# A cosformer attention and SwiGLU kernel: loads as casts on one queue, PSUM banks from one ring, the second batch woven into the first group, groups of 512 tokens

## The chip, the core and the metric

One Trainium2 chip, one NeuronCore. The metric is the device time of one execution in microseconds (us). The kernel before takes 384.12 us, the median of three runs (383.35 to 384.22).

## What is computed

```python
# q, k, v: [8 batches, 8 heads, 576 positions, 64], float32
q_p = concat(relu(q) * cos_w, relu(q) * sin_w)       # cos and sin of the position, 128 features
k_p = concat(relu(k) * cos_w, relu(k) * sin_w)
kv  = einsum('bhsf,bhsd->bhfd', k_p, v)
z   = sum(k_p, axis=2)
num = einsum('bhsf,bhfd->bhsd', q_p, kv)
x   = num / (einsum('bhsf,bhf->bhs', q_p, z) + 1e-6)  # -> 4608 tokens x 512
g   = x @ w_gate                                      # 512 x 1536
out = (silu(g) * (x @ w_val)) @ w_out                 # 1536 x 512, float32 out
```

## The kernel before

**Layout.** The 576 positions of a batch are cut into NC = 9 slots of 64 positions, slot c holding the positions p * 9 + c. The 8 heads go as 4 pairs g, one head of a pair on partitions 0 to 63, the other on 64 to 127. The 8 x 9 = 72 slots follow one another as the token axis of the feed-forward part. It is cut by `bounds` (L42) into nine groups: the first has 9 slots (576 tokens), seven have 8 (512 tokens), the last has 7 (448 tokens).

**Attention of one batch.** `relu` (L142) makes the relu of q and k as bf16 copies, `vcast` (L151) a bf16 copy of v, `vmul` (L156) multiplies v by the table of cosines and sines. `kv_mm` (L187) accumulates the kv products in PSUM (two calls of 36 matmuls), `kv_out` (L203) copies them out. q is transposed by DMA (`qturn_dma`, L168) or on TensorE (`qturn_pe`, L174). Then tiles of two slots (128 tokens; one slot where a group or the batch ends) are made: `a_half` (L220) makes four heads of a tile with four matmuls, an eviction on ScalarE (`tmp`, L239) and one on VectorE (`num`, L241), and there are ten halves to a batch; `x_norm` (L246) divides, with three VectorE operations; `x_turn` (L260) transposes the tile into `xT`, on TensorE and ScalarE if `fast`, else by a DMA transpose from SP's queue.

**Feed-forward of one group.** `ffn_fc` (L311) makes 128 of the 1536 hidden features for a range of tokens: four matmuls with w_gate and four with w_val into a pair of PSUM banks, Silu on ScalarE (`sg`), a product on VectorE into `ht` (L330). `ffn_out` (L336) makes 128 tokens of the output with twelve matmuls, an eviction that alternates between ScalarE and VectorE, and two stores from SP's queue.

**PSUM.** Three pools: `ps_f` has two buffers of two banks (feed-forward, transposes of q, the fast halves), `ps_o` two of one bank (outputs, transposes of x), `ps_a` one of two banks (kv products and all other halves).

**Order.** The program is emitted in the order in which each engine runs it. Batch 0's attention comes first (`features_fast(0)`, L355, then `tiles_fast`, L292). Batch 1's features (`features_fast(1)`) stand between the second and third output tile of group 0 (L417), and its tiles ahead of group 1. In groups 0 and 1 each `ffn_fc` is split into a first part of 4 slots (256 tokens) and the rest. The work of batches 2 to 7 is put into slots of a plan (`at`, L363): a group has 12 slots after its `ffn_fc` and 4 after its output tiles, SLOTS = 16. The table at L369 says at which slot of the plan the features of a batch begin and how many steps go into a slot, when q is transposed (`tq`), when the kv products are made (`tk`), and how many halves go into one slot (`hn`, from tk + 3 on).

**Loads.** k, v and q of batch 0 come as float32 by the queues of ScalarE and SP. A small copy on GpSimd (`hold`, L122) waits for q; behind it GpSimd's queue loads the weights, cast to bf16 by the DMA, and then batch after batch as float32 (two buffers per tensor).

Of the kernel before, what the change touches and what calls it, by code (L numbers as in the profile page):

```python
# [17 lines left out]
def kernel(  # L18
# [28 lines left out]
    raw = ctx.enter_context(tc.tile_pool(name="raw", bufs=2))  # L47
# [26 lines left out]

    load(0, "k", [nc.scalar], 2)
    load(0, "v", [nc.sync], 2)
    load(0, "q", [nc.scalar, nc.sync], 2)


    def angles(name, step):  # L80
        it = consts.tile([P, NC], mybir.dt.int32, name=f"{name}_i")
        for e in range(2):
            nc.gpsimd.iota(it[e * SH:(e + 1) * SH], pattern=[[1, NC]], base=e * step, channel_multiplier=NC)
        pos = consts.tile([P, NC], FP32, name=f"{name}_p")
        nc.vector.tensor_copy(out=pos, in_=it)
        return pos

    ident = consts.tile([P, P], BF16)
    pos_k = angles("k", 0)
    pos_t = angles("t", 1)  # L90
    halfpi = consts.tile([P, 1], FP32)
    nc.vector.memset(halfpi, math.pi / 2.0)
    zerob = consts.tile([P, 1], FP32)
    nc.vector.memset(zerob, 0.0)
    rad = math.pi / 2.0 / S
    csk = consts.tile([P, NC, 2], FP32)
    cst = consts.tile([P, NC, 2], FP32)
    for cs, pos in ((csk, pos_k), (cst, pos_t)):
        nc.scalar.activation(out=cs[:, :, 0], in_=pos, func=AF.Sin, scale=-rad, bias=halfpi[:])
        nc.scalar.activation(out=cs[:, :, 1], in_=pos, func=AF.Sin, scale=rad, bias=zerob[:])  # L100
    tiny = consts.tile([P, 1], FP32)
    nc.scalar.activation(out=tiny, in_=zerob, func=AF.Silu)
# [4 lines left out]
    )  # L107
    v2s = []
# [4 lines left out]
    make_identity(nc, ident)  # L113
# [5 lines left out]
    hold = consts.tile([P, 2], FP32)  # L119

    def load_weights():
        nc.gpsimd.tensor_copy(out=hold, in_=raws[0, "q"][:, 1:G:2, NC - 1, D - 1])  # L122
        wg_r = moe_w_gate.rearrange("(c p) f -> p c f", p=P)
        wv_r = moe_w_val.rearrange("(c p) f -> p c f", p=P)
        wo_r = moe_w_out.rearrange("(c p) f -> p c f", p=P)
        f0 = 0
        for n in (2, 2, 4, 4):
            fs = slice(f0 * P, (f0 + n) * P)
            f0 += n
            nc.gpsimd.dma_start(out=wg_sb[:, :, fs], in_=wg_r[:, :, fs])  # L130
            nc.gpsimd.dma_start(out=wv_sb[:, :, fs], in_=wv_r[:, :, fs])
        for i in range(3):
            cs = slice(4 * i, 4 * i + 4)
            nc.gpsimd.dma_start(out=wo_sb[:, cs], in_=wo_r[:, cs])
# [4 lines left out]
    def copy(i, out, in_):  # L139
        (nc.scalar.copy if i % 2 == 0 else nc.vector.tensor_copy)(out=out, in_=in_)  # L140

    def relu(b, nm, g, fast=False):  # L142
        if g == 0:
            st[b, nm] = rel.tile([P, J, NC, 2, D] if nm == "q" else [P, G, NC, D], BF16, name=f"r_{nm}")
        o = st[b, nm][:, g // 2, :, g % 2] if nm == "q" else st[b, nm][:, g]
        if fast:
            nc.vector.tensor_single_scalar(out=o, in_=raws[b, nm][:, g], scalar=0.0, op=ALU.max)  # L147
        else:
            nc.scalar.activation(out=o, in_=raws[b, nm][:, g], func=AF.Relu)  # L149

    def vcast(b, g, fast=False):  # L151
        t = rel.tile([P, NC, D], BF16, name="vb")
        st[b, "vb", g] = t
        (nc.gpsimd.tensor_copy if fast else nc.scalar.copy)(out=t, in_=raws[b, "v"][:, g])  # L154

    def vmul(b, g):  # L156
        nc.vector.tensor_tensor(  # L157
            out=v2s[b % 2][:, g, :, :, 0:D],
            in0=st.pop((b, "vb", g)).unsqueeze(2).to_broadcast([P, NC, 2, D]),
            in1=tab, op=ALU.mult,  # L160
        )
# [12 lines left out]
    def qturn_pe(b, j):  # L174
        qt = qt_of(b)
        ps = ps_f.tile([P, 2, 8, P], BF16, name="qt_ps", tag="f")
        for c in range(NC):
            nc.tensor.transpose(  # L178
                out=ps[:, c // 5, c % 5],
                in_=st[b, "q"][:, j, c].rearrange("p i d -> p (i d)"),  # L180
                identity=ident,
            )
        for i, (c0, n) in enumerate(((0, 5), (5, 4))):
            copy(i, qt[:, :, j, c0:c0 + n].rearrange("p e c s -> p c e s"),
                 ps[:, i, 0:n].rearrange("p c (e s) -> p c e s", e=2))

    def kv_mm(b, j):  # L187
        if j == 0:
            st[b, "kvps"] = ps_a.tile([P, 2, 512], FP32, name="kv_ps", tag="att")
        ps = st[b, "kvps"]  # L190
        for c in range(NC):
            for i in range(2):
                for e in range(2):
                    es = slice(e * SH, (e + 1) * SH)
                    g = 2 * j + i
                    nc.tensor.matmul(  # L196
                        out=ps[i * D:(i + 1) * D, e, j * 2 * D1:(j + 1) * 2 * D1],
                        lhsT=st[b, "k"][es, g, c],
                        rhs=v2s[b % 2][es, g, c, :, 0:D1],
                        start=(c == 0), stop=(c == NC - 1),  # L200
                    )

    def kv_out(b):  # L203
        kvs = kvp.tile([P, 2, J, 2 * D1], BF16, name="kvs")
        nc.scalar.copy(out=kvs.rearrange("p e j x -> p e (j x)"), in_=st.pop((b, "kvps"))[:, :, 0:J * 2 * D1])
# [4 lines left out]
    def tiles_of(b):  # L210
        cut = next((g - b * NC for g in bounds if b * NC < g < (b + 1) * NC), NC)
# [8 lines left out]
    def a_half(b, c, n, j, fast=False):  # L220
# [3 lines left out]
        ps = (ps_f if fast else ps_a).tile([P, 2, 512], FP32, name="a_ps", tag="f" if fast else "att")  # L224
        av = ps[0:m, :, 0:4 * D1].rearrange("p i (w e x) -> p i w e x", w=2, e=2)
# [9 lines left out]
        if j == 0:  # L235
            st[b, "num", c] = smp.tile([P, H, D1], FP32, name="num", bufs=3)
# [23 lines left out]
    def x_turn(b, c, n, fast=False):  # L260
        m = n * SH
        x = st.pop((b, "x", c))
        idx = b * NC + c
        tg = max(t for t in range(NTG) if bounds[t] <= idx)
        if tg not in xT:
            xT[tg] = xtp.tile([P, KC, 9 * SH], BF16, name="xT")
        off = (idx - bounds[tg]) * SH
        o = xT[tg][:, :, off:off + m]
        if fast:
            ps = ps_o.tile([P, KC, P], BF16, name="xt_ps", tag="o")  # L270
# [3 lines left out]
            nc.scalar.copy(out=o, in_=ps[:, :, 0:m])  # L274
        else:
            nc.sync.dma_start_transpose(out=o, in_=x[0:m])

    def features_fast(b):
        for g in range(G):
            vcast(b, g, fast=True)  # L280
        for g in range(G):
            relu(b, "k", g, fast=True)
            vmul(b, g)
        for j in range(J):
            kv_mm(b, j)
        for g in range(G):
            relu(b, "q", g)
        kv_out(b)
        for j in range(J):
            qturn_pe(b, j)  # L290

    def tiles_fast(b, fill):  # L292

        ts = tiles_of(b)
        fill = list(fill)
        for t, (c, n) in enumerate(ts):
            for j in range(J):
                a_half(b, c, n, j, fast=True)
            if t > 0:
                x_turn(b, *ts[t - 1], fast=True)  # L300
            x_norm(b, c, n)
            if t > 1:
                fill.pop(0)()
        x_turn(b, *ts[-1], fast=True)
        for f in fill:
            f()
# [4 lines left out]
    def ffn_fc(tg, fc, lo=0, hi=None, mid=None):  # L311

        hi = bounds[tg + 1] - bounds[tg] if hi is None else hi
# [3 lines left out]
        ps = ps_f.tile([P, 2, 512], FP32, name="f_ps", tag="f")  # L317
        for half, w in ((0, wg_sb), (1, wv_sb)):
            for kc in range(KC):
                nc.tensor.matmul(out=ps[:, half, 0:n], lhsT=w[:, kc, fs], rhs=xT[tg][:, kc, ts],  # L320
                                 start=(kc == 0), stop=(kc == KC - 1))
            if half == 0 and mid is not None:
                mid()
# [127 lines left out]
```

## Time and profile before

| | us |
|---|---|
| median of three runs | 384.12 |
| the profiled execution, as a run | 384.02 |
| its span, first to last instruction | 382.2 |
| TensorE busy in it | 339.3 (89%) |
| VectorE busy | 200.2 (52%) |
| ScalarE busy | 172.4 (45%) |
| GpSimd busy | 33.4 (9%) |

The span is what the trace shows; 1.8 us of the time lie around it. Matmuls are pipelined, so that the rows of one matmul overlap those of the next: the distance between two starts is its cost, not the duration printed. Idle time of an engine costs something only where the engine that ends the kernel waits for it. PE is TensorE, PEld its weight loads, DVE VectorE, ACT ScalarE, POOL GpSimd, SP the engine that issues stores and DMA transposes.

### The profile page before, as it was taken

What the parts mean: (1) busy time and instruction counts of PE and PEld (TensorE: products, weight loads), DVE (VectorE), ACT (ScalarE), POOL (GpSimd) and SP (SyncE); (2) the same over time, 40 slices, a digit from 0 to 9 for tenths busy, and PEclk for the clock granted to TensorE, in tenths of its full rate; (3) what the DMA queues carried; (4) which work ended last, traced back from release to release, by engine and by line L of the source; (5) the groups of instructions that cost most, each with busy time, mean ns of one, the idle gap of its engine ahead of it and who ended that gap; (6) DMA issues with size and microseconds to landing.
All of it is one profiled execution on the core that took longest, in us unless ns stands there. A gap on an engine that the chain in (4) does not pass through costs nothing.

```text
span 382.2 us, 6246 instructions
## 1 busy us (share of the span) xinstructions
PE 339.3 (89%) x2428; PEld 171.0 (45%) x2460; DVE 200.2 (52%) x461; ACT 172.4 (45%) x339; POOL 33.4 (9%) x54
## 2 busy tenths in 40 slices
PE   0679996858896789999999999999999999999995
PEld 0446663525673344344444444444444444444542
DVE  4564445275555654863595378447744753432321
ACT  3644333244754546743673376347533522321320
POOL 3842301200020020001001000000000000000000
PEclk9999999788998999999999999999999999999999
DMA  8899982740246378199219905501550133003013
GB/s 297 159 199 208 413 335 55 277 150 0 63 157 242 72 200 311 27 153 343 97 36 180 379 16 73 133 17 21 91 124 2 29 78 68 0 21 90 2 23 87
DMA packets 47981, 49.95 MB, mean 131 GB/s; under 512 B 30800, under 2 KB 36432, under 8 KB 47952
## 3 DMA queue, kind: packets, MB, share of 16 engines
q0 software_dynamic: 11568, 29.49, 25.2%
q1 hardware_dynamic: 35568, 18.29, 22.2%
q10 hardware_dynamic: 816, 1.77, 1.2%
q8 instruction: 19, 0.31, 0.3%
q14 instruction: 10, 0.08, 0.1%
HBM read 37.75 MB, written 9.44 MB: 123 GB/s over the span
## 4 chain that ended last, share of the span: by engine, by line
PE 81%; DVE 9%; ACT 4%; DMA 2%; issue 2%; ACTq 0%; DVEq 0%
PE f_ps L320 48%; PE o_ps L341 24%; PE a_ps L229 4%; PE kv_ps L196 3%; DVE ht L330 2%; DMA raw_k<-in_k_dram 2%; DVE v L157 2%; DVE num L241 2%; ACT sg L325 2%; DVE x L254 1%; PE qt_ps L178 1%; ACT tmp L239 1%; PE xt_ps L272 1%; DVE r_k L147 1%; DVE ob L140 1%
## 5 line engine op out<-in xcount | busy, mean ns | idle before, releaser
L330 DVE TENSOR_TENSOR ht<-sg,f_ps 128x192 bf16<-128x192 bf16 (+5 forms) x192 | 81.5, 451 | 100.4 <-ACT sg L325 100.2
L325 ACT ACTIVATE sg<-f_ps 128x512 bf16<-128x512 f32 (+3 forms) x132 | 68.5, 519 | 123.9 <-PE f_ps L320 109.3
L320 PE MATMUL f_ps<-xT,wg_sb 128*128 128x512 bf16 (+3 forms) x518 | 118.1, 348 | 6.1 <-DVE ht L330 3.8
L320 PE MATMUL f_ps<-xT,wv_sb 128*128 128x512 bf16 (+3 forms) x522 | 116.5, 347 | 0.0
L341 PE MATMUL o_ps<-wo_sb,ht 128*128 128x512 bf16 x416 | 97.6, 384 | 1.3 <-issue 0.6
L320 PEld LDWEIGHTS <-wv_sb 128*128 128x128 bf16 x528 | 52.9, 100 | 43.2
L320 PEld LDWEIGHTS <-wg_sb 128*128 128x128 bf16 x528 | 47.5, 100 | 46.2 <-DVE ht L330 7.2
L341 PEld LDWEIGHTS <-ht 128*128 128x128 bf16 x432 | 41.2, 99 | 49.7 <-issue 2.8
L241 DVE SCALAR_TENSOR_TENSOR num<-a_ps,cst,tmp 128x260 f32<-128x260 f32 (+1 forms) x80 | 38.2, 482 | 16.6 <-ACT tmp L239 16.2
L239 ACT ACTIVATE tmp<-a_ps,cst 128x260 f32<-128x260 f32 (+1 forms) x80 | 37.4, 473 | 20.6 <-PE a_ps L229 19.6
L229 PE MATMUL a_ps<-kvs,qt 64*128 64x130 bf16 (+1 forms) x320 | 24.7, 237 | 11.9 <-DVE num L241 8.2
L157 DVE TENSOR_TENSOR v<-vb,tab 128x1152 bf16<-128x1152 bf16 x32 | 25.9, 810 | 9.8 <-ACT vb L154 9.5
L140 DVE COPY ob<-o_ps 128x512 f32<-128x512 f32 x18 | 12.4, 690 | 35.2 <-PE o_ps L341 35.2
L229 PEld LDWEIGHTS <-qt 64*128 64x128 bf16 (+1 forms) x320 | 11.4, 99 | 39.8 <-issue 37.2
L254 DVE TENSOR_TENSOR x<-num,rec 128x512 bf16<-128x512 f32 (+1 forms) x40 | 27.6, 690 | 1.4
L140 ACT COPY ob<-o_ps 128x512 f32<-128x512 f32 x18 | 10.5, 585 | 37.9 <-PE o_ps L341 35.7
L196 PE MATMUL kv_ps<-v,r_k 64*64 64x130 bf16 x576 | 14.6, 241 | 14.6 <-DVE v L157 14.6
L149 ACT ACTIVATE r_q<-raw_q 128x576 bf16<-128x576 f32 x32 | 20.7, 676 | 6.0 <-DMA raw_q<-in_q_dram 6.0
L196 PEld LDWEIGHTS <-r_k 64*64 64x64 bf16 x576 | 11.7, 119 | 20.2 <-issue 10.5
L73 POOL DMA_DIRECT2D raw_k<-in_k_dram x8 | 5.9, 741 | 133.0 <-ACT r_k L149 127.2
L149 ACT ACTIVATE r_k<-raw_k 128x576 bf16<-128x576 f32 x24 | 16.3, 677 | 0.0
L154 ACT CAST vb<-raw_v 128x576 bf16<-128x576 f32 x24 | 16.0, 667 | 0.0
(39 smaller groups left out, 83.1 us busy)
## 6 DMA issues: line engine op xcount, KB each, us to landing
out_dram<-ob SPq DMA_DIRECT2D x72, 128.0 KB, 2.4
raw_k<-in_k_dram POOLq DMA_DIRECT2D x6, 1152.0 KB, 6.9
raw_v<-in_v_dram POOLq DMA_DIRECT2D x6, 1152.0 KB, 9.0
raw_q<-in_q_dram POOLq DMA_DIRECT2D x6, 1152.0 KB, 11.3
wo_sb<-in_moe_w_out_dram POOLq DMA_DIRECT2D x3, 512.0 KB, 18.0
raw_k<-in_k_dram ACTq DMA_DIRECT2D x2, 576.0 KB, 6.7
raw_v<-in_v_dram SPq DMA_DIRECT2D x2, 576.0 KB, 6.4
raw_k<-in_k_dram POOLq DMA_DIRECT2D x2, 576.0 KB, 18.4
```

What stands on the lines that cost most here:

```text
L140: (nc.scalar.copy if i % 2 == 0 else nc.vector.tensor_copy)(out=out, in_=in_)
L149: nc.scalar.activation(out=o, in_=raws[b, nm][:, g], func=AF.Relu)
L157: nc.vector.tensor_tensor(out=v2s[b % 2][:, g, :, :, 0:D], in0=st.pop((b, "vb", g)).unsqueeze(2).to_broadcast([P, NC, 2, D]), in1=tab, op= ...
L196: nc.tensor.matmul(out=ps[i * D:(i + 1) * D, e, j * 2 * D1:(j + 1) * 2 * D1], lhsT=st[b, "k"][es, g, c], rhs=v2s[b % 2][es, g, c, :, 0:D1] ...
L229: nc.tensor.matmul(out=av[:, i, :, e], lhsT=qt[hs, e, j, c:c + n].rearrange("p c s -> p (c s)"), rhs=kvs[hs, e, j].rearrange("p (w x) -> p ...
L239: nc.scalar.activation(out=tmp[0:m], in_=av[:, :, 0].rearrange("p i e x -> p i (e x)"), func=AF.Copy, scale=cst[0:m, c, 0:1])
L241: nc.vector.scalar_tensor_tensor(out=nv, in0=av[:, :, 1].rearrange("p i e x -> p i (e x)"), scalar=cst[0:m, c, 1:2], in1=tmp[0:m], op0=ALU ...
L254: nc.vector.tensor_tensor(out=x[0:m].rearrange("p (h d) -> p h d", h=H), in0=num[0:m, :, 0:D], in1=rec[0:m].to_broadcast([m, H, D]), op=AL ...
L320: nc.tensor.matmul(out=ps[:, half, 0:n], lhsT=w[:, kc, fs], rhs=xT[tg][:, kc, ts], start=(kc == 0), stop=(kc == KC - 1))
L325: nc.scalar.activation(out=sg[:, 0:n], in_=ps[:, 0, 0:n], func=AF.Silu)
L330: nc.vector.tensor_tensor(out=ht[:, fc, r:r + w], in0=sg[:, at_:at_ + w], in1=ps[:, 1, at_:at_ + w], op=ALU.mult)
L341: nc.tensor.matmul(out=o_ps, lhsT=ht[:, fc, r:r + P], rhs=wo_sb[:, fc], start=(fc == 0), stop=(fc == FC - 1))
```

## The change

- Groups are 8 slots each (`GH`), all nine of 512 tokens. `ht` holds two groups.
- k, v and q are loaded as bf16, cast by the DMA, all from GpSimd's queue with three buffers per tensor; only k of batch 0 comes as float32 from SP's queue. The order on GpSimd's queue is: v of batch 0, q of batch 0 (slots 0 to 3, then 4 to 8), weights of `ffn_fc` 0 to 7, k of batch 1, weights of 8 to 11, v of batch 1, the first slots of q of batch 1, w_out, the rest of q of batch 1, batch 2. `hold` and `vcast` are gone, and the relu of k is made in place.
- All of PSUM is one tile of 8 banks. `take` gives them out in a ring, one or an aligned pair at a time, and skips banks that are held (kv products until copied out, outputs until complete).
- `qturn_pe` transposes raw q, and its eviction makes the relu.
- For batch 0 two tiles are made ahead of the first `ffn_fc`, two more between the first six half-width `ffn_fc` of group 0, the last in group 0's slots 2 to 4. Only group 0 is split into halves of 256 tokens.
- Batch 1's features stand in slots 3 to 11 of group 0; its first eight halves, their turns and the rest of q's transposes stand between thirds of group 0's four output tiles; its last tile is in group 1.
- For batch 2, `hn` goes from 2 to 1, and the features of a batch are 8 steps and no longer 12.

```diff
-    bounds = [0, 9] + [9 + 8 * i for i in range(1, 8)] + [NH]
-    NTG = len(bounds) - 1
-    R = 6 * P
+    GH = 8
+    T = GH * SH
+    NTG = NH // GH
+    R = 2 * T
...
+    banks = psum.tile([P, 8, 512], FP32, name="banks")
+    bank_at = [0]
+    held = {}
+    def take(n, hold=None):
+        while True:
+            b0 = (bank_at[0] + n - 1) // n * n % 8
+            bank_at[0] = b0 + n
+            if not any(b0 <= x < b0 + n for r in held.values() for x in r):
+                break
+        if hold is not None:
+            held[hold] = range(b0, b0 + n)
+        return banks[:, b0] if n == 1 else banks[:, b0:b0 + n]
...
+    def load(b, nm, parts=1):
+        t, sv, n = raw_of(b, nm), source(b, nm), G // parts
+        for i in range(parts):
+            sl = slice(i * n, (i + 1) * n)
+            nc.gpsimd.dma_start(out=t[:, sl].rearrange("p g c d -> p g (c d)"), in_=sv[:, sl])
...
+    def qturn_pe(b, j, lo, hi, eng):
+        ps = take(1).bitcast(BF16).rearrange("p (c x) -> p c x", x=P)
+        for c in range(lo, hi):
+            for i in range(2):
+                nc.tensor.transpose(out=ps[i * D:(i + 1) * D, c - lo], in_=raws[b, "q"][:, 2 * j + i, c],
+                                    identity=ident)
+        relu_op(eng, qt_of(b)[:, :, j, lo:hi].rearrange("p e c s -> p c e s"),
+                ps[:, 0:hi - lo].rearrange("p c (e s) -> p c e s", e=2))
...
-        ps = ps_f.tile([P, 2, 512], FP32, name="f_ps", tag="f")
+        if 2 * n <= 512:
+            both = take(1)
+            ps = [both[:, 0:n], both[:, n:2 * n]]
+        else:
+            ps = [take(1)[:, 0:n] for _ in range(2)]
...
+    for i in range(4):
+        load_w(i)
+    load(1, "k")
+    load_w(4)
+    load_w(5)
+    load(1, "v", 2)
+    load_slots(1, "q", 0, CA)
+    for i in range(3):
+        load_wo(i)
+    load_slots(1, "q", CA, NC)
     load_next(2)
...
+    for i in range(2):
+        relu_k(0, 2 * i, 2 * i + 2, "dve")
+    vmul(0, 0)
+    vmul(0, 1)
+    kv_mm(0, 0)
+    vmul(0, 2)
+    qturn_pe(0, 0, 0, CA, "act")
+    vmul(0, 3)
+    qturn_pe(0, 1, 0, CA, "act")
+    kv_mm(0, 1)
+    kv_out(0, ("act", "dve"))
+    ts = tiles_of(0)
+    for t in range(2):
+        for j in range(J):
+            a_half(0, *ts[t], j)
+        x_norm(0, *ts[t])
+    for j in range(J):
+        qturn_pe(0, j, CA, NC, "act")
+    for t in range(2):
+        x_turn(0, *ts[t], fast=True)
...
-            2: (s0 + 1, 2, s0 + 4, s0 + 7, 2),
+            2: (s0 + 1, 2, s0 + 4, s0 + 7, 1),
             3: (s0 - 6, 2, s0 - 3, s0 + 1, 1),
         }.get(b, (s0 - 13, 1, s0 - 7, s0 + 1, 1))
...
+    for f, fns in enumerate(early):
+        ffn_fc(0, f, 0, HALF)
+        for fn in fns:
+            fn()
+    for f in range(FC):
+        ffn_fc(0, f, HALF, GH)
+        if f + len(early) < FC:
+            ffn_fc(0, f + len(early), 0, HALF)
+        slot(f)
+    for piece in range(3):
+        for t in range(OUT):
+            ffn_out(t, 4 * piece, 4 * piece + 4)
+            for fn in sub.pop((piece, t), ()):
+                fn()
+    x_turn(1, *ts1[3], fast=True)
+    load_next(3)
...
+    for tg in range(1, NTG):
+        s0 = SLOTS * tg
+        for fc in range(FC):
+            ffn_fc(tg, fc)
+            slot(s0 + fc)
+        for i in range(OUT):
+            ffn_out(tg * OUT + i)
+            slot(s0 + FC + i)
```

## Rows read from the trace of the kernel before

**Rows 1.** The page's 40 equal slices: TensorE's busy tenths and granted clock

```profile
PE   0679996858896789999999999999999999999995
...
PEclk9999999788998999999999999999999999999999
```

**Rows 2.** Windows, a stretch of groups 0 and 1 and a later one

```profile
core 0: us, PE busy (x) PEld busy (x) DVE busy (x) ACT busy (x) POOL busy (x), PEclk, DMA share, GB/s
...
74.00:112.00 38.00, 29.55 (x274) 20.30 (x273) 21.44 (x60) 21.28 (x48) 2.23 (x3) 0.91 0.27 91
...
188.00:226.00 38.00, 37.74 (x265) 16.21 (x268) 23.93 (x56) 21.05 (x40) 2.25 (x3) 1.00 0.57 153
```

**Rows 3.** The chain that ended last: start us, us, what

```profile
1.24 7.92 DMA raw_k<-in_k_dram
...
22.84 1.88 PE f_ps L320 x8
...
57.56 4.93 PE o_ps L341 x22
...
137.99 3.45 PE f_ps L320 x16
...
174.06 3.45 PE f_ps L320 x16
177.51 0.65 PE kv_ps L196 x35
...
318.03 10.14 PE f_ps L320 x47
...
349.11 18.16 PE f_ps L320 x96
367.32 10.32 PE o_ps L341 x47
```

**Rows 4.** DMA in two windows (columns as in rows 2)

```profile
5.00:10.00 5.00, 1.33 (x36) 1.31 (x36) 3.87 (x7) 0.99 (x2) 2.37 (x4) 1.00 1.04 411
25.00:30.00 5.00, 3.84 (x31) 2.49 (x29) 3.37 (x8) 2.78 (x7) 1.41 (x3) 1.00 1.24 206
```

**Rows 5.** Timeline, half-width blocks of group 0, early and later

```profile
22.84 1.01 PE L320 MATMUL f_ps<-xT,wg_sb 128*128 128x256 bf16 x4 [0.67 <-ACT xT L274]
...
35.40 0.60 PE L320 MATMUL f_ps<-xT,wg_sb 128*128 128x256 bf16 x4
...
35.83 0.60 PE L320 MATMUL f_ps<-xT,wv_sb 128*128 128x256 bf16 x4
```

**Rows 6.** The page's costliest groups: the product of v with the table

```profile
L157 DVE TENSOR_TENSOR v<-vb,tab 128x1152 bf16<-128x1152 bf16 x32 | 25.9, 810 | 9.8 <-ACT vb L154 9.5
```

**Rows 7.** Timeline, one half of a tile behind an output tile, to its x

```profile
204.40 0.29 PE L229 MATMUL a_ps<-kvs,qt 64*128 64x130 bf16 x4
...
205.24 0.49 DVE L241 SCALAR_TENSOR_TENSOR num<-a_ps,cst,tmp 128x260 f32<-128x260 f32 x1
...
206.21 0.69 DVE L254 TENSOR_TENSOR x<-num,rec 128x512 bf16<-128x512 f32 x1
```

**Rows 8.** The tile xT: its DMA transposes, issue to landing

```profile
DMA to landing us min/median/max: 2.3/2.4/12.6
```

**Rows 9.** The page's DMA issues: q of batches 2 to 7

```profile
raw_q<-in_q_dram POOLq DMA_DIRECT2D x6, 1152.0 KB, 11.3
```

**Rows 10.** Windows around the three falls of the granted clock (columns as in rows 2)

```profile
65.00:73.00 8.00, 5.94 (x93) 4.76 (x94) 4.13 (x7) 1.98 (x3) 3.18 (x5) 0.57 0.52 166
82.00:90.00 8.00, 6.02 (x44) 3.55 (x45) 5.22 (x15) 3.37 (x8) 0.00 (x0) 0.57 0.00 0
120.00:124.00 4.00, 3.67 (x14) 1.44 (x15) 1.55 (x4) 1.62 (x3) 0.00 (x0) 0.57 0.31 57
```

**Rows 11.** Timeline, the last group's first output tile beside the last product into ht

```profile
367.32 1.89 PE L341 MATMUL o_ps<-wo_sb,ht 128*128 128x512 bf16 x8
367.88 0.62 DVE L330 TENSOR_TENSOR ht<-sg,f_ps 128x448 bf16<-128x448 bf16 x1 [0.89 <-ACT sg L325]
```

More of the change, by code (lines that the diff above doesn't have):

```diff
@@ new lines @@
+    k32 = consts.tile([P, G, NC, D], FP32)
+    for i in range(2):
+        sl = slice(2 * i, 2 * i + 2)
+        nc.sync.dma_start(out=k32[:, sl].rearrange("p g c d -> p g (c d)"), in_=source(0, "k")[:, sl])
+    pos_i = consts.tile([P, NC], mybir.dt.int32)
+    nc.gpsimd.iota(pos_i, pattern=[[1, NC]], base=0, channel_multiplier=NC)
+    CA = 4
+    load(0, "v", 2)
+    load_slots(0, "q", 0, CA)
+    load_slots(0, "q", CA, NC)
+    rad = math.pi / 2.0 / S
+    bias = consts.tile([P, 2, 2], FP32)
@@ L107 @@
     )
+    ident = consts.tile([P, P], BF16)
+    make_identity(nc, ident)
     v2s = []
@@ L118 @@
     wo_sb = consts.tile([P, FC, d_model], BF16)
[L119 to L134, printed above, removed]
@@ L151, in vcast, with load_w @@
[L151 to L154, printed above, removed]
+    wg_r = moe_w_gate.rearrange("(c p) f -> p c f", p=P)
+    wv_r = moe_w_val.rearrange("(c p) f -> p c f", p=P)
+    wo_r = moe_w_out.rearrange("(c p) f -> p c f", p=P)
+    def load_w(i):
+        fs = slice(2 * i * P, (2 * i + 2) * P)
+        nc.gpsimd.dma_start(out=wg_sb[:, :, fs], in_=wg_r[:, :, fs])
+        nc.gpsimd.dma_start(out=wv_sb[:, :, fs], in_=wv_r[:, :, fs])
@@ L172, in qturn_dma @@
         )
[L174 to L185, printed above, removed]
+    def qturn_pe(b, j, lo, hi, eng):
[6 more added lines that the diff above has]
+                ps[:, 0:hi - lo].rearrange("p c (e s) -> p c e s", e=2))
     def kv_mm(b, j):
         if j == 0:
-            st[b, "kvps"] = ps_a.tile([P, 2, 512], FP32, name="kv_ps", tag="att")
+            st[b, "kvps"] = take(2, ("kv", b))
         ps = st[b, "kvps"]
@@ L210, in tiles_of @@
     def tiles_of(b):
-        cut = next((g - b * NC for g in bounds if b * NC < g < (b + 1) * NC), NC)
+        cut = next((g - b * NC for g in range(0, NH + 1, GH) if b * NC < g < (b + 1) * NC), NC)
         res = []
@@ L262, in x_turn @@
         x = st.pop((b, "x", c))
-        idx = b * NC + c
-        tg = max(t for t in range(NTG) if bounds[t] <= idx)
+        tg, off = divmod(b * NC + c, GH)
         if tg not in xT:
-            xT[tg] = xtp.tile([P, KC, 9 * SH], BF16, name="xT")
-        off = (idx - bounds[tg]) * SH
-        o = xT[tg][:, :, off:off + m]
+            xT[tg] = xtp.tile([P, KC, T], BF16, name="xT")
+        o = xT[tg][:, :, off * SH:off * SH + m]
         if fast:
-            ps = ps_o.tile([P, KC, P], BF16, name="xt_ps", tag="o")
+            ps = take(1).bitcast(BF16).rearrange("p (k x) -> p k x", x=P)
             for kc in range(KC):
@@ L273, in x_turn, with ffn_fc @@
                                     identity=ident[0:m, 0:m])
-            nc.scalar.copy(out=o, in_=ps[:, :, 0:m])
+            nc.scalar.copy(out=o, in_=ps[:, 0:KC, 0:m])
         else:
             nc.sync.dma_start_transpose(out=o, in_=x[0:m])
[L278 to L306, printed above, removed]
     ht = consts.tile([P, FC, R], BF16, name="ht")
-    def ffn_fc(tg, fc, lo=0, hi=None, mid=None):
-        hi = bounds[tg + 1] - bounds[tg] if hi is None else hi
+    def ffn_fc(tg, fc, lo=0, hi=GH):
         n = (hi - lo) * SH
@@ L321, in ffn_fc @@
                                  start=(kc == 0), stop=(kc == KC - 1))
-            if half == 0 and mid is not None:
-                mid()
-        sg = sgp.tile([P, 512], BF16, name="sg")
-        nc.scalar.activation(out=sg[:, 0:n], in_=ps[:, 0, 0:n], func=AF.Silu)
-        t0, at_ = (bounds[tg] + lo) * SH, 0
-        while at_ < n:
-            r = (t0 + at_) % R
-            w = min(n - at_, R - r)
-            nc.vector.tensor_tensor(out=ht[:, fc, r:r + w], in0=sg[:, at_:at_ + w],
-                                    in1=ps[:, 1, at_:at_ + w], op=ALU.mult)
-            at_ += w
@@ L334, with ffn_out @@
-    out_v = out.rearrange("(b p c) f -> b c p f", p=SH, c=NC)
-    def ffn_out(t):
-        o_ps = ps_o.tile([P, d_model], FP32, name="o_ps", tag="o")
+        sg = sgp.tile([P, T], BF16, name="sg")
+        nc.scalar.activation(out=sg[:, 0:n], in_=ps[0], func=AF.Silu)
+        r = (tg * T + lo * SH) % R
+        nc.vector.tensor_tensor(out=ht[:, fc, r:r + n], in0=sg[:, 0:n], in1=ps[1], op=ALU.mult)
+    out_v = out.rearrange("(b p c) f -> b c p f", p=SH, c=NC)
+    o_ps = {}
+    def ffn_out(t, f0=0, f1=None):
+        f1 = FC if f1 is None else f1
+        if f0 == 0:
+            o_ps[t] = take(1, ("o", t))
@@ L339, in ffn_out @@
         r = (t * P) % R
[L340 to L341 removed]
+        for fc in range(f0, f1):
+            nc.tensor.matmul(out=o_ps[t], lhsT=ht[:, fc, r:r + P], rhs=wo_sb[:, fc],
                              start=(fc == 0), stop=(fc == FC - 1))
+        if f1 < FC:
+            return
+        ps = o_ps.pop(t)
+        held.pop(("o", t))
         ob = obp.tile([P, d_model], FP32, name="ob")
[L344 removed]
+        if t == NH // 2 - 1:
+            hd = d_model // 2
+            nc.scalar.copy(out=ob[:, 0:hd], in_=ps[:, 0:hd])
+            nc.scalar.copy(out=ob[:, hd:], in_=ps[:, hd:])
+        else:
+            (nc.scalar.copy if t % 2 == 0 else nc.vector.tensor_copy)(out=ob, in_=ps)
@@ L416 @@
             slot(s0 + FC + i)
-            if tg == 0 and i == 1:
-                features_fast(1)
-                load_next(3)
     assert not plan, sorted(plan)
```

187 lines of the change are left out of this document (101 added, 86 removed).

## The prediction

> **What bounds the kernel now.** I read the slices first, then two windows, then the chain of waits. In the slices [rows 1] TensorE is full from about the fifteenth slice on and has holes before; the granted clock falls below full in the same early part. The windows say it in numbers [rows 2]: in the later stretch TensorE is busy 37.74 of 38 us, VectorE 23.93 and ScalarE 21.05, so TensorE bounds it and nothing that only unloads other engines helps there; in the early stretch it is busy 29.55 of 38 though no other engine is full. The chain [rows 3] gives the stages: the first feed-forward matmul starts at 22.84, group 0's outputs at about 57.1 (its first piece in the chain at 57.56), group 2 at 137.99, group 3 at 174.06, group 7 at 318.03, the last at 349.11, its outputs at 367.32. From here a group with one batch's attention costs 36.07 us (137.99 to 174.06) and one without it 31.08 (318.03 to 349.11), that is 144 matmuls at 0.2158 us. Groups 0 and 1 take 115.15 us (22.84 to 137.99) for 1088 tokens; at the later pace they would take about 75. That is the part to be won, and the change works in it.
>
> **The sum, part by part.** It is made on the profiled execution's own time, 384.02 us (span 382.2 and 1.8 around it); the median of the runs is 0.10 above.
>
> *Start.* Before, k's second half holds the chain until 1.24 + 7.92 = 9.16 [rows 3], because k and v, 2.36 MB, come together at 411 GB/s [rows 4], 5.7 us. Now k goes first and alone on SP's queue and v follows through GpSimd: 1.18 MB take 2.9 us, so k is there at 6.3 without sharing, 7.7 if v shares half of it; I take 6.6. From there to the first feed-forward matmul the same chain stands (relu, v products, kv products, halves, a norm, a turn): 13.7 us before. It loses GpSimd's casts of v and gets one longer wait, both relus of k ahead of the first v product; I add 0.4. First matmul at 20.7, gain 2.1 (bounds: 0, if k is no earlier, to 4). Casting costs the transfers nothing: 206 GB/s of bf16 written [rows 4] are 412 read. In the new order the last `ffn_fc` weights come behind 9.8 MB, 24 us at that rate after about 6, at 30, and w_out behind 4.8 MB more, at 42; they are wanted at some 38 and 50. GpSimd's queue, past which all of this moves, has no other work that someone waits for.
>
> *Clock.* At 22.84 eight matmuls of 256 take 1.88 us [rows 3] and a row of four 1.01; at 35.40 a four starts 0.43 after the last and has a row of 0.60 [rows 5]: 1.2 and 2.4 GHz, though the slices grant full speed in both places [rows 1]. In between TensorE was busy 3.84 of 5 us [rows 4]. At most (35.40 - 22.84) / 2 = 6.3 was lost; now the blocks are queued almost without a hole, and I take 5 us at the low rate, 2.5 lost (bounds 0 to 6.3).
>
> *Group 0, `ffn_fc`.* 24 half-width blocks by 0.86 (two of 0.43) are 20.7. Between them lie batch 0's last six halves, three turns, batch 1's kv products and 16 narrow transposes. A batch costs TensorE 36.07 - 31.08 = 5.0, of which two kv calls are 1.3 (0.65 for 35 matmuls) [rows 3], so a half costs (5.0 - 1.3) / 10 = 0.37; a turn of four 128-column transposes is four quarters of 0.2158 and a wait, 0.3; a narrow transpose 0.055. Together 2.2 + 0.9 + 1.3 + 0.9 = 5.3. One wait of 1 us remains, for the fourth tile's turn ahead of the second halves. With the clock's 2.5: 29.5, so the outputs start at 50.2. The VectorE work set between them is hidden as long as it fits: per pair of blocks 1.72 us on TensorE stand beside two products of some 0.4 and one v product of 0.81 [rows 6].
>
> *Group 0's outputs with batch 1.* 48 matmuls are 10.4, eight halves 3.0, three turns 0.9, 20 narrow transposes 1.1, and 1 us of small waits: 16.4. Then the fourth tile's turn stands right ahead of group 1. From the start of a half to the end of its x are 2.50 us, from 204.40 to 206.90 [rows 7], with the turn (0.3) and an eviction of about 0.5 that is 3.3, less the half's own 0.37: 2.9 us idle. Group 1 starts at 69.5. This replaces 57.1 to the end of `features_fast(1)` and `tiles_fast(1)`.
>
> *Group 1.* Full-width blocks: 31.1, kv 1.3, eight halves 3.0 (batch 1's last two, batch 2's first six), a turn 0.3: 35.7, to 105.2. With VectorE and ScalarE 24 and 21 of 38 busy under one batch [rows 2], batch 3's products (4 by 0.81) on top leave them below TensorE, and the ring lets them lag by up to four blocks.
>
> *The seam into group 2.* This is a new wait. With one half to a slot, batch 2's sixth half comes in the last slot of group 1, and group 2's first matmul needs its x, turned by DMA. Half to x 2.50 [rows 7], the DMA transpose 2.4 [rows 8], less 0.3: 4.6 us in which TensorE has nothing; all of group 2 is queued behind it. A transpose can take up to 12.6 [rows 8] if batch loads are in flight, which need 11.3 us [rows 9]; but GpSimd issues batch 5 as soon as batch 2's kv products free the buffer, some 17 us ahead, so I take the median. On SP's queue only the output tile's two stores stand ahead, whose eviction is done before x. After such a hole the clock falls: 1.2 GHz is granted for 3.4 to 6.9 us at a time [rows 10], since a mean of 0.57 over 4 or 8 us is 86% of it at half. I take the short one, 1.7 lost (bounds 0 to 3.4). Group 2 starts at 111.5, against 137.99: 26.5 won.
>
> *Rest.* Group 2 has two halves more, +0.7. Groups 3 to 7 are bound by TensorE and keep their matmuls: nothing (the ring could only win the 0.26 us idle in 38). The last group has 512 tokens for 448: 96 by 0.2158 less 18.2, +2.5. The last eviction is split on ScalarE instead of whole on VectorE: nothing either way beyond 0.2.
>
> Sum: 384.02 - 26.5 + 0.7 + 2.5 = 360.7; with 0.1 to the median, 360.8.
>
> **Rivals.**
> (a) *The seam is covered*: the tail of group 1 hides it and the clock holds. 360.8 - 4.6 - 1.7 = 354.5. Against it: TensorE takes its work in order, and nothing stands between. 0.13.
> (b) *The clock swings.* Before, three spells at 1.2 GHz, 17.2 us in all, came after TensorE had been waiting [rows 10], 8.6 lost; the change keeps several short waits in the same stages. If as much is lost again on top of the start, it is 6.9 more: 367.7. 0.15. The Trainium skill (TensorE: Matmul & The Clock Gate, section "A second HAM failure mode: psum-queue depth-cycling") says that a kernel that cycled through PSUM banks each iteration idled briefly between groups of matmuls and had its clock swing between the two rates, which speaks against a ring. By that rule this rival would be the forecast. The trace so far does not bear it out where blocks follow each other: the later stretch cycles two buffers and was granted 1.00 [rows 2].
> (c) *The consumers still bind* in groups 0 and 1. If TensorE's early share of 29.55 in 38 [rows 2] stayed, the 80 us of its work up to 105 would take 103, and nearly all of the gain were gone; with half of that, 372. Against it: before, a block waits for a pair of banks two blocks back; now four. 0.09.
> (d) *One tile, one lock: slower.* All banks are one tile. If it were guarded as a whole, every block would wait for the Silu and product of the one before, 1.2 us (367.32 to 368.50) [rows 11], by 96 full-width blocks 115 us: 476. It decides from 0.24 us a block on, which eats the 23 won. Against it: `ht` is one tile too, and an output matmul reads it while a product writes elsewhere in it [rows 11]. 0.03.
>
> **How the numbers follow.** Forecast 0.60, (a) 0.13, (b) 0.15, (c) 0.09, (d) 0.03. The range takes in (a) and (b) with the bounds of start, clock and seam, and half of (c)'s way: 353 to 371. A measurement here can tell about 0.3% from no change, 1.2 us. All cases but (d) and the far end of (c) are faster by more: 0.96 faster, 0.01 the same, 0.03 slower.
>
> **What would show it.** In the changed profile: first feed-forward matmul near 20.7, outputs of group 0 near 50, group 1 near 69.5 and group 2 near 111 in the chain, with a DMA transpose of x and 4 to 5 us of idle TensorE right ahead of it; steady groups still 36; no wait for weights. Wrong: idle TensorE on `ht` or `sg` inside group 1 (then (c)), low clock after 75 other than behind the seam (then (b)), no wait at the seam (then (a)), or a DMA ahead of TensorE in groups 0 and 1.

## The result and the profile after

The changed kernel takes 365.15 us, the median of four runs (362.56 to 365.67), against 383.87 us for the kernel before in the same comparison; the ratio is 0.950, 95% interval 0.946 to 0.954. The forecast was 360.8, in a range of 353 to 371. The profiled execution took 362.56 us with a span of 360.4, so it is one of the short ones; an execution of the more usual length comes with the first experiment.

TensorE's slices and granted clock on the page of the changed kernel, beside [rows 1]:

```profile
PE   0678999699956999999999999999999999999994
...
PEclk9879999999996999999999999999999999999999
```

Fewer holes, and two places below full clock. The windows of [rows 2], 74 to 112 and 188 to 226 (columns: us, busy of PE, PEld, DVE, ACT, POOL with counts, granted clock, DMA share, GB/s):

```profile
74.00:112.00 38.00, 30.98 (x226) 13.61 (x225) 20.79 (x39) 18.27 (x34) 2.23 (x3) 0.94 0.64 116
188.00:226.00 38.00, 38.00 (x300) 16.49 (x299) 22.55 (x45) 18.31 (x34) 0.00 (x0) 1.00 0.32 65
```

The later stretch is full, as before. The early one holds one large hole now instead of many small ones. The chain, beside [rows 3] (start us, us, what; L312 is `ffn_fc`, L329 `ffn_out`):

```profile
19.07 1.86 PE banks L312 x8
...
50.01 0.97 PE banks L329 x4
...
68.59 1.89 PE banks L312 x8
...
108.62 2.45 DMA xT<-x
111.12 3.58 PE banks L312 x8
...
149.88 3.45 PE banks L312 x16
185.79 3.45 PE banks L312 x16
...
293.53 20.72 PE banks L312 x96
314.25 10.36 PE banks L329 x48
324.61 20.72 PE banks L312 x96
```

The feed-forward starts at 19.07 instead of 22.84, group 2 at 111.12 instead of 137.99. A group with one batch's attention costs 35.91 (149.88 to 185.79), one without it 31.08 (293.53 to 324.61), so almost nothing was won behind group 2. What was won lies ahead of it, 26.9 us; some 5 of them are given back behind, by the low clock after the hole, two more halves in group 2 and the longer last group. And 7 us ahead of group 2 are still a hole, with a DMA transpose of x as the step before it. SP's issues ahead of that hole (timeline: start us, us, engine, line, operation, tiles, count), TensorE's first row behind it, and VectorE's row for the last x that group 2 needs:

```profile
100.50 1.20 SPq L295 DMA_TRANSPOSE xT<-x  x1
101.80 3.47 SPq L189 DMA_TRANSPOSE qt<-r_q  x2
105.36 3.17 SPq L344 DMA_DIRECT2D out_dram<-ob  x4
108.62 1.25 SPq L295 DMA_TRANSPOSE xT<-x  x1
...
111.12 1.89 PE L312 MATMUL banks<-xT,wg_sb 128*128 128x512 bf16 x4 [7.01 <-DMA xT<-x]
...
105.62 0.69 DVE L275 TENSOR_TENSOR x<-num,rec 128x512 bf16<-128x512 f32 x1
```

That x was done at 106.31. Its transpose was issued at 108.62, because SP was still issuing batch 3's two transposes of q and four stores, and landed at 111.07. The four matmuls behind the hole take 1.89 us and not 1.03: the clock had fallen (a window, columns as above).

```profile
110.00:115.00 5.00, 3.88 (x13) 1.24 (x14) 0.20 (x1) 0.64 (x2) 0.00 (x0) 0.54 0.10 21
```

### The profile page after: what moved, and what is told of

Same layout as the page of the kernel before. It is cut to its first block, busy times and chain, and to the rows that moved or that the text cites. A ratio compares the mean times of both kernels' runs of the same rounds, so it can differ in the third digit from the quotient of the medians.

```text
span 360.4 us, 6121 instructions
## 1 busy us (share of the span) xinstructions
PE 329.9 (92%) x2400; PEld 154.0 (43%) x2400; DVE 189.0 (52%) x386; ACT 157.2 (44%) x301; POOL 33.3 (9%) x49
## 4 chain that ended last, share of the span: by engine, by line
PE 87%; DVE 4%; DMA 3%; SPq 2%; ACT 2%; issue 1%; POOL 0%; ACTq 0%; POOLq 0%
PE banks L312 53%; PE banks L329 25%; PE banks L250 5%; PE banks L212 3%; DMA raw_q<-in_q_dram 2%; DVE x L275 2%; DVE num L262 1%; SPq L189 1%; SPq L344 1%; PE banks L291 1%; PE banks L198 1%; DMA xT<-x 1%; ACT tmp L260 1%; DVE rec L273 0%; ACT xT L293 0%
## 5 line engine op out<-in xcount | busy, mean ns | idle before, releaser
L317 DVE TENSOR_TENSOR ht<-sg,banks 128x512 bf16<-128x512 bf16 (+1 forms) x120 | 75.7, 632 | 98.8 <-PE banks L312 82.7
L312 PE MATMUL banks<-xT,wg_sb 128*128 128x512 bf16 (+1 forms) x480 | 115.3, 363 | 8.8 <-DMA xT<-x 7.0
L312 PE MATMUL banks<-xT,wv_sb 128*128 128x512 bf16 (+1 forms) x480 | 114.5, 361 | 0.0
L315 ACT ACTIVATE sg<-banks 128x512 bf16<-128x512 f32 (+1 forms) x120 | 66.5, 554 | 94.2 <-PE banks L312 93.7
L329 PE MATMUL banks<-wo_sb,ht 128*128 128x512 bf16 x432 | 98.9, 380 | 0.0
L312 PEld LDWEIGHTS <-wv_sb 128*128 128x128 bf16 x480 | 47.5, 99 | 47.5 <-issue 1.1
L312 PEld LDWEIGHTS <-wg_sb 128*128 128x128 bf16 x480 | 42.2, 98 | 49.5 <-DMA xT<-x 7.2
L329 PEld LDWEIGHTS <-ht 128*128 128x128 bf16 x432 | 39.8, 98 | 46.7
L260 ACT ACTIVATE tmp<-banks,cst 128x260 f32<-128x260 f32 (+1 forms) x80 | 37.8, 477 | 42.4 <-PE banks L250 42.4
L262 DVE SCALAR_TENSOR_TENSOR num<-banks,cst,tmp 128x260 f32<-128x260 f32 (+1 forms) x80 | 38.5, 483 | 15.7 <-ACT tmp L260 15.2
L341 DVE COPY ob<-banks 128x512 f32<-128x512 f32 x17 | 11.8, 691 | 37.7 <-PE banks L329 36.2
L250 PE MATMUL banks<-kvs,qt 64*128 64x130 bf16 (+1 forms) x320 | 23.1, 227 | 1.1 <-ACT ob L341 0.7
L177 DVE TENSOR_TENSOR v<-raw_v,tab 128x1152 bf16<-128x1152 bf16 x32 | 23.5, 751 | 0.7 <-DMA raw_v<-in_v_dram 0.7
L250 PEld LDWEIGHTS <-qt 64*128 64x128 bf16 (+1 forms) x320 | 9.7, 96 | 32.8 <-issue 30.9
L162 ACT ACTIVATE raw_k<-raw_k 128x576 bf16<-128x576 bf16 x24 | 15.8, 675 | 0.0
```

Source lines behind the costliest of these rows:

```text
L162: nc.scalar.activation(out=out, in_=in_, func=AF.Relu)
L177: nc.vector.tensor_tensor(out=v2s[b % 2][:, g, :, :, 0:D], in0=raws[b, "v"][:, g].unsqueeze(2).to_broadcast([P, NC, 2, D]), in1=tab, op=AL ...
L250: nc.tensor.matmul(out=av[:, i, :, e], lhsT=qt[hs, e, j, c:c + n].rearrange("p c s -> p (c s)"), rhs=kvs[hs, e, j].rearrange("p (w x) -> p ...
L260: nc.scalar.activation(out=tmp[0:m], in_=av[:, :, 0].rearrange("p i e x -> p i (e x)"), func=AF.Copy, scale=cst[0:m, c, 0:1])
L262: nc.vector.scalar_tensor_tensor(out=nv, in0=av[:, :, 1].rearrange("p i e x -> p i (e x)"), scalar=cst[0:m, c, 1:2], in1=tmp[0:m], op0=ALU ...
L312: nc.tensor.matmul(out=o, lhsT=w[:, kc, fs], rhs=xT[tg][:, kc, ts], start=(kc == 0), stop=(kc == KC - 1))
```

## The experiments

Each run was timed in three rounds beside the kernel before (383.87 to 384.47 us in the four comparisons). The first theory was that the ring, the weaving and the order fill groups 0 and 1, and that the hole at the seam between groups 1 and 2 gives a part back. Each recorded expectation names its own theory A and its rival B.

**The changed kernel again.** No edit.

> The changed kernel as it is, once more. It was seen at 362.6 us in the profiled execution and at about 365 in four others, with a higher mean granted clock in the longer ones. Theory A (the hole at the start of group 2 varies with what stands on SP's queue and with where the clock falls): this profile shows the stages up to group 2 and after it as before within 0.3 us, and only the hole and the cold blocks behind it differ, by up to 3 us. Rival B (the start varies): the first feed-forward matmul moves from 19.1 by 1 us or more.

Measured: 364.33 us (363.18 to 365.16), the profiled span 363.3. Neither held. The hole is 7.1 us, the same; the start moved by 0.7, to 19.80. The larger part of the 2.9 us between the two spans is the start of group 1: at 69.65 its first eight matmuls take 3.17 us, and 1.89 in the first profile, behind the same two waits. TensorE's rows and the chain here, then the same window here and in the first profile:

```profile
68.91 0.29 PE L291 MATMUL banks<-ident,x 64*128 64x64 bf16 x4 [1.90 <-DVE x L275]
69.65 1.46 PE L312 MATMUL banks<-xT,wg_sb 128*128 128x512 bf16 x4 [0.46 <-ACT xT L293]
...
69.65 3.17 PE banks L312 x8
```

```profile
64.00:74.00 10.00, 6.91 (x38) 2.63 (x37) 5.23 (x13) 3.54 (x8) 0.00 (x0) 0.83 0.98 218
```

```profile
64.00:74.00 10.00, 7.53 (x50) 3.28 (x50) 5.33 (x12) 5.20 (x12) 0.00 (x0) 1.00 0.99 220
```

A mean of 0.83 over 10 us is 3.4 us at the low rate, 1.7 lost. So the short waits ahead of group 1 let the clock fall in one execution and not in another. The record of the granted clock alone can mislead: at the start of this run it grants full speed where eight matmuls of 256 columns take 1.87 us and not 0.86. That is why the mean granted clock is higher here (0.986 and 0.981), though the run is longer.

```profile
19.80 1.87 PE banks L312 x8
...
19.80:21.80 2.00, 2.00 (x12) 1.15 (x11) 0.00 (x0) 0.10 (x1) 1.16 (x2) 1.00 1.46 198
```

**Two halves to a slot for batch 2.**

```diff
-            2: (s0 + 1, 2, s0 + 4, s0 + 7, 1),
+            2: (s0 + 1, 2, s0 + 4, s0 + 7, 2),
```

> Batch 2's halves go two to a slot again, so that its sixth half is made three slots earlier and the last x of group 2 is turned behind output tile 4 and not 7. Theory A (the hole ahead of group 2 is the latency from the last half to the landing of its DMA transpose, 7.0 us, plus some 1.75 lost at the low clock behind it): no idle TensorE at the start of group 2, clock 1.00 there, 8.8 us less than the changed kernel. Rival B (two halves to a slot bring the waits of the kernel before back, which had 78% of TensorE busy in that stretch, or SP's queue is late anyway): not over 3 us less.

Measured: 354.48 us (353.41 to 355.95), ratio to the kernel before 0.924 (0.921 to 0.927). Theory A. The chain passes from the outputs into group 2 without a transfer, and the window holds no idle time:

```profile
106.12 3.62 PE banks L312 x16
```

```profile
100.00:110.00 10.00, 9.95 (x80) 4.54 (x83) 8.65 (x19) 4.49 (x9) 0.00 (x0) 1.00 0.82 144
```

Group 2 starts at 106.12 (113.86 in the run above) at full clock. One digit of the change had cost some 10 us.

**Batch 3's transposes of q later.**

```diff
-            3: (s0 - 6, 2, s0 - 3, s0 + 1, 1),
+            3: (s0 - 6, 2, s0 + 1, s0 + 1, 1),
```

> Only batch 3's two DMA transposes of q move, from the second output slot of group 1 to the second slot of group 2; the halves of batch 2 stay one to a slot. Theory A (of the 7.0 us of idle TensorE 2.3 are SP's queue: x was done at 106.31 and its transpose began at 108.62, behind two transposes of q and four stores): the hole shrinks to 4.7 us and the time by 2 to 2.5 us, more if the clock then does not fall. Rival B (the transposes themselves are slow on the transfer engines): the transpose begins at once but lands no earlier, and nothing changes.

Measured: 378.03 us. The seam did what theory A said, and the time went up by 13 to 14 us against the two medians of the changed kernel. Waits of TensorE (waiting for, total us, times, longest), the chain, and the issues from GpSimd and SP behind the seam:

```profile
PE banks L250 <- DMA qt<-r_q: 12.8, 2, 7.9
...
PE banks L312 <- DMA xT<-x: 4.8, 1, 4.8
```

```profile
108.19 2.40 DMA xT<-x
...
122.45 15.17 DMA qt<-r_q
```

```profile
121.10 3.78 SPq L189 DMA_TRANSPOSE qt<-r_q  x2
121.34 0.74 POOL L93 DMA_DIRECT2D raw_k<-in_k_dram  x1 [30.12 <-ACT tmp L260]
122.07 0.76 POOL L93 DMA_DIRECT2D raw_v<-in_v_dram  x1
122.80 0.77 POOL L93 DMA_DIRECT2D raw_q<-in_q_dram  x1
```

The hole shrank from 7.0 to 4.8, so 2.2 of it were SP's queue. But the moved transposes now fell among batch 6's loads: the second landed 15.17 us after its issue, at 137.6, just after q of batch 6 (issued at 122.80, landed 14.6 later), and TensorE waited for them.

**The kernel before with groups of 512 alone.**

```diff
-    bounds = [0, 9] + [9 + 8 * i for i in range(1, 8)] + [NH]
+    bounds = list(range(0, NH + 1, 8))
```

> The kernel before with only its groups cut at every 8 slots (512 tokens each) and nothing else. Theory A (the size of the groups by itself moves work from the first to the last group and saves a little of the stalls of the split blocks): within 2 us of the kernel before. Rival B (the even cut carries the gain, since it removes odd block widths): 375 or less.

Measured: 381.35 us, ratio 0.994 (0.992 to 0.996). A small gain, just outside A's 2 us and far from B: the cut carries about 2.5 of the 19 us.

**Three pools again.** From here on the base is the version with two halves to a slot (354.48). The core of the edit:

```diff
+        if kind == "a":
+            return banks[:, 6:8]
+        if kind == "o" and t is not None and t < 4:
+            return banks[:, t]
+        turn[kind] += 1
+        if kind == "f":
+            b0 = turn[kind] % 2 * 2
+            return banks[:, b0] if n == 1 else banks[:, b0:b0 + 2]
+        return banks[:, 4 + turn[kind] % 2]
```

> Built on the version with two halves to a slot (354.5 us). The banks are given out as in the kernel before: two pairs for the feed-forward blocks, the transposes of q and batch 0's halves, two banks for outputs and turns (while batch 1 is woven in, the four outputs lie in the feed-forward banks), one pair for the kv products and all other halves. Theory A (the ring is what fills groups 0 and 1: a block waits no longer for the product two blocks back): TensorE waits for ht again in group 0 (about 0.35 us per pair of blocks, 4 us), in the four feature slots of group 1 (2 us) and for num in the outputs of group 0 (2 us); about 362 us. Rival B (the weaving and the order alone fill them, two pairs would do): within 1.5 us of 354.5.

Measured: 366.75 us, 12.3 more. Theory A had the sign, not the place:

```profile
PE banks L250 <- DVE num L262: 9.9, 13, 1.7
```

TensorE waits ahead of halves (L250) for the eviction of the half before, and never for `ht` ahead of a block. Group 1, where two halves share a slot, takes 45.00 us (71.00 to 116.00) and 36.97 in the base (69.15 to 106.12), which is 8.0 of the 12.3. So a theory C: what the ring gives is a second pair of banks for the halves.

**No weaving.** Batch 1's tiles stand behind group 0's outputs.

```diff
     for piece in range(3):
         for t in range(OUT):
             ffn_out(t, 4 * piece, 4 * piece + 4)
+    for piece in range(3):
+        for t in range(OUT):
             for fn in sub.pop((piece, t), ()):
                 fn()
```

> Built on the version with two halves to a slot (354.5 us). Batch 1's eight halves, their turns and the second part of q's transposes stand behind group 0's four output tiles and no longer between their thirds. Theory A (between the thirds they cost only their matmuls, alone they run at VectorE's pace, 8 by 0.49 and 4 by 1.1 us and a start and an end of 2 to 3): from the start of the outputs to group 1 some 3 us more, and the clock falls in it, 2 more; 358 to 361 us. Rival B (the weaving only moves the work): within 1 us of 354.5.

Measured: 360.55 us, 6.1 more. Theory A, at the upper end: in this run's chain the outputs start at 51.23 and group 1 at 74.68,

```profile
51.23 10.47 PE banks L329 x48
...
74.68 3.58 PE banks L312 x8
```

23.5 us, where the changed kernel takes 18.6 (50.01 to 68.59); 3.58 us for eight matmuls is the low clock again.

**Weights ahead of batch 1.**

```diff
-    for i in range(4):
+    for i in range(6):
         load_w(i)
+    for i in range(3):
+        load_wo(i)
     load(1, "k")
-    load_w(4)
-    load_w(5)
     load(1, "v", 2)
     load_slots(1, "q", 0, CA)
-    for i in range(3):
-        load_wo(i)
     load_slots(1, "q", CA, NC)
```

> Built on the version with two halves to a slot (354.5 us). On GpSimd's queue all weights go ahead of batch 1, as in the kernel before; casts, buffers and everything else stay. Theory A (the order of need has slack: batch 1's k would land near 39 and v near 42, and they are wanted from 38 and 41 on): VectorE waits by 1 us or so in slots 3 to 5 of group 0, the ring covers it, within 1 us of 354.5. Rival B (without this order batch 1 comes too late to be woven into group 0, and the gain hangs on it): 358 us or more.

Measured: 354.73 us, 0.3 more, within the spread. Theory A: the order of need on the queue decides nothing that can be seen here.

**No hole ahead of group 1.** The second part of batch 1's q is transposed in group 0's last slot, which frees the second third of the outputs for the last four halves.

```diff
-    at(11, lambda: qturn_pe(1, 1, 0, CA, "act"))
+    at(11, lambda: (qturn_pe(1, 1, 0, CA, "act"), qturn_pe(1, 0, CA, NC, "act"), qturn_pe(1, 1, CA, NC, "act")))
...
+        sub[1, i] = [lambda c=c, n=n, j=j: a_half(1, c, n, j)]
...
+    sub[1, 0].append(lambda: x_turn(1, *ts1[0], fast=True))
+    sub[1, 2].append(lambda: x_turn(1, *ts1[1], fast=True))
+    sub[2, 0] = [lambda: x_turn(1, *ts1[2], fast=True)]
+    sub[2, 2] = [lambda: x_turn(1, *ts1[3], fast=True)]
```

> The version with two halves to a slot (354.5 us), and the second part of batch 1's q is transposed in group 0's last slot, so that all eight halves lie between the first two thirds of the outputs and all four turns are done before the last third ends. Theory A (the hole ahead of group 1, some 2.9 us from the last half to its turn, and the blocks at the low clock behind it, 1.6 us, are the last ones that order can fill): no idle TensorE over 1 us at the start of group 1, clock 1.00 there, 350 to 351.5 us. Rival B (VectorE then bounds the two thirds with the halves): the same idle time lies between the halves, 354 to 355 us.

Measured: 351.05 us (350.87 to 351.71), ratio 0.914 (0.912 to 0.916), the fastest of all. Theory A:

```profile
66.57 1.73 PE banks L312 x8
```

Group 1 starts 2.0 us earlier than in the changed kernel (2.6 earlier than in the base, 69.15) and at full clock, and the runs lie within 0.8 us of each other, where the version before this edit spread over 2.5.

**Two pairs for the blocks, a ring of four banks for the rest.** Outputs go round the blocks' four banks.

```diff
+        if kind == "f":
+            turn["f"] += 1
+            b0 = turn["f"] % 2 * 2
+            return banks[:, b0] if n == 1 else banks[:, b0:b0 + 2]
+        if kind == "o":
+            turn["o"] += 1
+            return banks[:, turn["o"] % 4]
```

> Built on the version with two halves to a slot (354.5 us). Feed-forward blocks have two fixed pairs, as in the kernel before; outputs go round the same four banks; halves, kv products and transposes go round the other four. With three pools the time was 366.8 and TensorE waited 9.9 us for num ahead of a half and never for ht ahead of a block. Theory C (what the ring gives is the second pair for the halves; for the blocks two pairs do): 354 to 356.5 us, the waits of halves for num under 2 us. Rival A (the depth for the blocks counts, hidden in that run behind the other wait): 358 us or more, with waits of blocks for ht.

Measured: 365.58 us, which is A's number, for a reason of the edit itself:

```profile
PE banks L332 <- DVE ht L320: 9.3, 9, 1.5
```

L332 is the output matmul: the first output of a group took a bank of the last block and waited for its product, about once a group. Blocks did not wait, and halves waited 0.9 us. It settles nothing, so it was mended:

```diff
-            return banks[:, turn["o"] % 4]
+            return banks[:, (2, 3, 0, 1)[(turn["o"] - 1) % 4]]
```

> The version with two fixed pairs for the blocks and a ring of the other four banks (365.6 us), in which the first output of each group took the bank of the last block and waited 9.3 us in all for its product; here the outputs begin in the other pair. Theory C (for the blocks two pairs do; the ring's worth is the second pair for the halves): no such wait, 354 to 356.5 us. Rival A (depth for the blocks counts): waits of blocks for ht come up in groups 0 and 1, 358 us or more.

Measured: 355.05 us (352.63 to 355.17), 0.6 from the ring of eight. Theory C: no wait of TensorE for `ht` is left in the list, and two pairs are enough for the blocks.

**Three pools in the changed kernel itself** (one half to a slot; the edit as above). Batch 2's last halves and batch 3's kv products share the one pair at the same time here, so those products are overwritten and the output of batch 3 is another; the order of the work stays.

> The changed kernel (365 us, one half to a slot for batch 2) with its banks given out by the three pools and nothing else undone. Theory C (a single pair costs where two halves of a tile follow each other in one slot; one to a slot, the eviction is done before the next): 365 to 368 us, about half of what three pools cost with two halves to a slot (12 us) or less. Rival A (the ring carries groups 0 and 1 whatever the slots hold): 373 us or more.

Measured: 370.44 us, 5.3 to 6.1 above the two medians of the changed kernel, between the two theories. TensorE's waits:

```profile
PE banks L309 <- DMA xT<-x: 7.1, 1, 7.1
...
PE banks L250 <- DVE num L262: 3.1, 8, 0.9
PE banks L213 <- DVE num L262: 2.2, 2, 1.1
```

The single pair costs 5.3 us (3.1 ahead of halves, 2.2 ahead of kv products) and the seam stays as it was: half of what it costs with two halves to a slot, as C says, though the time is above its bound of 368.

**What was not separated.** The even cut on the kernel before (2.5), and the ring (12.3) and the weaving (6.1), each taken back from the version with two halves to a slot, make 20.9 of the 29.4 us between these two kernels, if they simply add. The loads as casts and the new order at the start were not taken back by themselves, so what each of them is worth stays open.

## Why the prediction was right

The time lay in the range, 4.3 us above the value. Some of the agreement in between is luck, since misses cancelled. By its own steps:

- *Start*: 20.7 forecast, 19.07 and 19.80 measured. k alone on its queue was there by 5.9 and not 6.6, but k no longer held the start: VectorE waited for v and began its product at 7.39 in the first profile and 8.02 in the second. From there to the first feed-forward matmul it is 11.7 and 11.8 us, so v's landing makes most of the 0.7 between the two starts. The step "the same chain stands" from k was wrong, on the safe side.

```profile
7.39 2.84 DVE L177 TENSOR_TENSOR v<-raw_v,tab 128x1152 bf16<-128x1152 bf16 x4 [0.72 <-DMA raw_v<-in_v_dram]
```

- *Clock at the start*: 2.5 us were taken as lost. The windows of the first profile are below; 0.56 and 0.76 are 4.4 and 2.4 us at the low rate, half of them ahead of the first feed-forward matmul at 19.07. Behind it some 3.4 us at the low rate are left, 1.7 lost for 2.5.

```profile
15.00:20.00 5.00, 2.15 (x14) 1.47 (x14) 2.60 (x7) 2.23 (x4) 2.21 (x4) 0.56 1.45 196
20.00:25.00 5.00, 4.24 (x33) 2.35 (x31) 2.54 (x7) 2.33 (x6) 2.64 (x4) 0.76 1.32 203
```

- *Group 0 and its outputs*: outputs forecast at 50.2, found at 50.01; group 1 at 69.5, found at 68.59 and 69.65. The first agreement is luck: the start came 1.6 us early, and group 0 took 30.9 us for 29.5, because TensorE waited 2.8 us for batch 0's later tiles where one wait of 1 us was taken (its waits from 19.07 to 50, and a row of the timeline). The outputs with batch 1 took 18.6 for 19.3, with 2.4 us of idle TensorE ahead of group 1 where 2.9 were taken.

```profile
PE banks L291 <- DVE x L275: 2.1, 3, 1.2
...
30.30 0.60 PE L312 MATMUL banks<-xT,wg_sb 128*128 128x256 bf16 x4 [0.67 <-ACT xT L293]
```

- *Group 1*: forecast to end at 105.2, it ended at 104.1; it took 35.5 us for 35.7.
- *The seam*: the mechanism was right, the size not: 4.6 us forecast, 7.0 and 7.1 measured. The step that failed is "On SP's queue only the output tile's two stores stand ahead". Two transposes of q and two more stores stood there, since SP issues in order and takes 1.2 to 2.1 us for each transpose. With the q transposes moved away the hole was 4.8. The loads did not reach it, as argued: q of batch 5, issued at 88.61, had landed at 98.80.
- *Clock behind the seam*: 1.7 taken, and the first eight matmuls show it: 3.58 us for 1.83.
- *What was left out of the sum*: the clock can fall in the 3 us ahead of group 1 too, 1.7 us. The second profile, an execution of 365.11 us and so close to the median, shows it: group 1 begins at 69.65 (0.15 late), takes 37.1 us for 35.7, and the hole 7.1 for 4.6. That is 4.1 of the 4.4 us by which this execution lies above the 360.7 of the sum. In the first profile the clock held there, and the time is 1.9 above.
- *Rest*: steady groups 35.91 for 36.07, groups without attention 31.08: right.

Of the rivals, (a) fell: the hole is there, and the run without it is 10 us faster. (b) had a piece of the truth, one more spell at the low clock, but not its size. The Trainium skill (TensorE: Matmul & The Clock Gate, section "A second HAM failure mode: psum-queue depth-cycling") tells of a kernel that cycled through PSUM banks, idled briefly between groups of matmuls and had its clock swing. Here the ring went round with TensorE busy 38.00 of 38 us at a granted 1.00 (188 to 226): the cycling alone did not lower the clock, and the idle time that the page tells of beside it was not there. (c) and (d) fell: no wait of a block for a bank is in the list of TensorE's waits, and TensorE was busy through all of group 1 and all that follows the hole (the two stretches of the first profile, columns as in [rows 2]).

```profile
68.59:104.10 35.51, 35.51 (x252) 15.49 (x251) 20.74 (x38) 21.15 (x39) 2.23 (x3) 1.00 0.66 123
111.12:355.00 243.88, 243.88 (x1582) 105.61 (x1583) 127.71 (x248) 102.72 (x189) 4.46 (x6) 0.99 0.35 66
```

One reason the forecast gave against (c) was wrong though the number was not touched by it: the four blocks of depth. Two pairs do; the ring's worth, 12 us with two halves to a slot, is that a half finds a second pair. And the loads' order, which the sum costed at nothing, was shown to be worth nothing that can be told from the spread (0.3 us).

## What to carry to other kernels

After a weave, read each seam: the last piece of work that the next group's first matmul needs, and everything that the queue which carries it must issue first; here one slot's difference was worth 10 us, half as much as the whole change. When banks are pooled, ask which waiter gets the new bank: it was the small evictions between the blocks, not the blocks. And a transfer that is moved out of one queue's way has to be placed against the loads of the other queues too.

## What had not been expected of the hardware

- A DMA transpose of q that is issued beside the loads from GpSimd's queue lands only as they end: 4.0 to 4.9 us in the changed kernel, and 15.17 us, in the run with batch 3's transposes later, beside three loads (1.18 MB read and 0.59 written each) that were issued within 2 us of it, landing 0.2 us after the last of them. The Trainium skill (DMA: Bandwidth & Descriptors, section "Queues, rings and completion order") says that each transfer engine goes round between the queues it has work for, packet by packet. In the main the packets agree with it: from 125 to 138 GpSimd's queue (q0) moved 1535 packets and SP's (q1) 1504, one for one, but SP's carry only a fifth of the bytes. SP's two transposes in that time, q's second and the next x, thus have nearly as many packets as the three loads, and end with them. What the rule does not explain are the first 3 us, in which SP's queue moved 28 packets and GpSimd's 444. The queues (packets, MB, share of 16 engines) from 125 to 138, then from 125 to 128:

```profile
q0 software_dynamic: 1535, 1.71, 82.9%
q1 hardware_dynamic: 1504, 0.36, 24.3%
...
q0 software_dynamic: 444, 0.50, 109.6%
q1 hardware_dynamic: 28, 0.00, 1.3%
```

- The clock can fall over a wait of 1.9 us with a short turn and a wait of 0.5 behind it, as ahead of group 1, and whether it does changes from one execution to the next of the same kernel; that alone made 1.7 of the 2.9 us between the spans of the two profiles.
